# Turning the summed probabilities of two key blocks instead of each one

## The chip, the cores and the metric

The kernel runs on one core of a Trainium2 chip. The metric is the time of the device in microseconds (us), the median of several runs. A profiled execution gives the rows shown here; in them PE is TensorE (PEld its weight loads), DVE is VectorE, ACT is ScalarE, POOL is GpSimd and SP issues DMAs.

## The reference

Three parts follow each other. The first is attention with a sliding window of 128 keys and 4 sink keys, over 4 batches x 8 heads, 768 positions, 64 columns a head:

```python
rel = pos[:, None] - pos[None, :]
keep = (pos[None, :] < n_sink) | ((rel >= 0) & (rel < window))
a = softmax(where(keep, scale * q @ k.T, -1e9))
x = a @ v                                   # to 3072 tokens x 512
h = x @ w_in;  x = (h * cos(h)) @ w_out     # 512 -> 2048 -> 512
```

Then a top-1 mixture of 8 experts: each token is routed by `argmax(x @ w_gate + bias)`, goes through `relu(x @ w1[e]) @ w2[e]` (512 to 1024 to 512) of its expert, and is scaled by its gate.

## The kernel before, in words

**Attention.** It is cut into 8 half-sequences (`hb`; `half = hb % 2`, the batch is `hb // 2`) of 384 queries, and each of these into 4 pairs of heads (`pr`). A half-sequence has three tiles `t` of 128 queries. A query's window lies in two neighbouring blocks of 128 keys: of the earlier block the keys behind a diagonal count, of its own block those up to the diagonal, so that the two parts are opposite triangles. Sixteen columns for the sinks stand between them: a tile of probabilities `Pb[t][j]` (`j` is the head of the pair) is `[earlier block 128 | sinks 16 | own block 128]`, 272 wide (`SEG` = 144, `W3` = 272). The first tile of a first half has no earlier block, and in the second tile of a first half (and in the first one) the sinks are within the blocks, by the masks with index 0 and 1.

`attn_front` loads q, k and v and turns q and k (`pq`, `pk`). Its `mid` makes the scores on TensorE (`ps`), adds the mask and takes the maximum on VectorE (L512), and exponentiates on ScalarE (L528), which also gives the row sums `sm`. Its `rest` scales `Pb` by 1/sum from the third half-sequence on (`whole`; L140 on VectorE, and on GpSimd for `hb` = 2), turns each 128x128 block with TensorE against the identity into the PSUM tile `pt` (L551 the earlier block, L552 the own one), and ScalarE copies `pt` to `pT` in SBUF (L554). The sinks' columns are gathered (`pc`), turned (`pz`) and copied (`sp`). Then `po` gathers the product with v: block by block of keys, two tiles of queries at a time, `pT` as the moving operand. ScalarE and VectorE part `po` into a high and a low half, `xT_h` and `xT_l`.

**The feed-forward part.** It works on the half-sequences one step behind: for each of 16 column blocks `f` twelve matmuls make `hp` (L136), VectorE and ScalarE make `ch` = h cos h from it, ScalarE the high half `g_h`, GpSimd the low half `g_l`, and nine matmuls add to `y` (L622). `hp` has two PSUM banks.

**The order.** Attention and feed-forward are generators. Each `yield` of attention returns a weight, and `run_ffn` advances the other generator by it. A scheduler then sets the order on each engine from this order and its own picture of durations. PSUM tiles named by `ps_a` (`pq`, `pk`, `ps`, `pt`, `pz`, `po`, `yT` and others) share a few banks in turn, so that a new one waits until the reader of an old one is done. Each engine executes its queue in order. The mixture of experts follows from about 800 us on, after the routing; it is not touched.

Of the kernel before, what the change touches and what calls it, by code (L numbers as in the profile page):

```python
# [13 lines left out]
BF16 = DT.bfloat16  # L14
# [3 lines left out]
ALU = mybir.AluOpType  # L18
AX = mybir.AxisListType

P = 128
# [40 lines left out]
def kernel(  # L62
# [30 lines left out]
    SEG = P + NS  # L93
    W3 = 2 * P + NS
# [7 lines left out]
    PE, ACT, DVE, POOL, SP = nc.tensor, nc.scalar, nc.vector, nc.gpsimd, nc.sync  # L102
# [30 lines left out]
    const = ctx.enter_context(tc.tile_pool(name="const", bufs=1))  # L133

    def mm(o, l, r, start, stop):
        PE.matmul(o, l, r, start=start, stop=stop)  # L136

    def ts(e, o, i, s1, op0, s2=None, op1=None):
        if op1 is None:
            e.tensor_scalar(out=o, in0=i, scalar1=s1, scalar2=None, op0=op0)  # L140
        else:
            e.tensor_scalar(out=o, in0=i, scalar1=s1, scalar2=s2, op0=op0, op1=op1)  # L142
# [4 lines left out]
    def tt(e, o, a, b, op):  # L147
        e.tensor_tensor(out=o, in0=a, in1=b, op=op)  # L148


    ident = const.tile([P, P], F32, name="ident")
# [162 lines left out]
    def steps(hb):  # L314
        return STEPS_0 if hb <= 1 else STEPS_1
# [80 lines left out]
    def attn_front(hb, pr):  # L396
        b, half = divmod(hb, 2)
# [3 lines left out]
        extra = hb <= EX and pr % 2 == 1  # L401

        whole = hb > EX
        vs_n, sp = vs_n2[pr % 2], sp2[pr % 2]
        n_ps = [0]

        def psb(name):
            if hb > 0 or not extra:
                return ps_a(name)
            n_ps[0] += 1  # L410
            return ps_y(n_ps[0] % NQ, name)
# [119 lines left out]
        def rest():  # L531
            xh, xl = xT[hb]
            for t in range(NQ if whole else 0):
                ts(DVE, sm[:, 2 * t:2 * t + 2], sm[:, 2 * t:2 * t + 2], 1e-9, ALU.add)
                DVE.reciprocal(sm[:, 2 * t:2 * t + 2], sm[:, 2 * t:2 * t + 2])
                for j in range(2):
                    c0, c1, _ = cols(t)
                    i = 2 * t + j
                    if hb < NPOOL:
                        ts(POOL, Pb[t][j][:, c0:c1], Pb[t][j][:, c0:c1], sm[:, i:i + 1], ALU.mult, 0.0, ALU.add)  # L540
                    else:
                        ts(DVE, Pb[t][j][:, c0:c1], Pb[t][j][:, c0:c1], sm[:, i:i + 1], ALU.mult)
            yield steps(hb)[3]
            pT = apool.tile([P, 2, NQ * 256], F32, name="pT", bufs=2)
            for t in range(NQ):
                pt = psb("pt").rearrange("p (j x) -> p j x", j=2)
                first = half == 0 and t == 0
                s0 = P if first else 0
                for j in range(2):
                    if not first:  # L550
                        PE.transpose(pt[:, j, 0:P], Pb[t][j][:, 0:P], ident)  # L551
                    PE.transpose(pt[:, j, P:2 * P], Pb[t][j][:, SEG:W3], ident)  # L552
                o_ = slice(t * 256 + s0, (t + 1) * 256)
                ACT.activation(out=pT[:, :, o_], in_=pt[:, :, s0:256], func=AF.Copy)  # L554
                yield steps(hb)[4]
            if not whole:

                ts(DVE, sm, sm, 1e-9, ALU.add)
                DVE.reciprocal(sm, sm)
                rb = [pb_x[t + NQ * (pr % 2)][:, 3 * P:4 * P] for t in range(NQ)]  # L560
                for t in range(NQ):
                    POOL.tensor_copy(rb[t].rearrange("p (j d) -> p j d", d=D),
                                     sm[:, 2 * t:2 * t + 2].unsqueeze(2).to_broadcast([P, 2, D]))
            t0 = 2 if half == 0 else 0
            pc = apool.tile([P, NQ, 2, NS], F32, name="pc")
            if extra:
                for t in range(t0, NQ):
                    for j in range(2):
                        POOL.tensor_copy(pc[:, t, j], Pb[t][j][:, P:SEG])
            else:  # L570
                (POOL if hb < NPOOL else DVE).tensor_copy(pc[:, t0:], Pt[:, t0:, :, P:SEG])
            pz = psb("pz")
            for t in range(t0, NQ):
                PE.transpose(pz[0:2 * NS, t * P:(t + 1) * P], pc[:, t].rearrange("p j s -> p (j s)"), ident)
            ACT.activation(out=sp[0:2 * NS, t0 * P:], in_=pz[0:2 * NS, t0 * P:HALF], func=AF.Copy)
            yield steps(hb)[5]
            def band(blk):

                own = blk if half == 0 else blk - 1
                ta, tb = max(own, 0), min(own + 1, NQ - 1)  # L580
                c0 = ta * P
                c1 = (tb + 1) * P
                m0 = own * 256 + P if own >= 0 else 0
                return c0, c1, m0, m0 + (c1 - c0)

            po = psb("po")
            for j in range(2):
                mm(po[hr[j], t0 * P:HALF], vs_n[:, j * D:(j + 1) * D], sp[:, t0 * P:HALF], True, False)
            for blk in range(nblk):
                c0, c1, m0, m1 = band(blk)  # L590
                for j in range(2):
                    mm(po[hr[j], c0:c1], vn[:, blk, j, :], pT[:, j, m0:m1], False, blk == nblk - 1)
            yield 2 * nblk * steps(hb)[6]
            if whole:
                ACT.activation(out=xh[:, pr, :], in_=po[:, 0:HALF], func=AF.Copy)
                tt(DVE, xl[:, pr, :], po[:, 0:HALF], xh[:, pr, :].bitcast(F32), ALU.subtract)
            else:
                pf = psb("pf")
                for t in range(NQ):
                    mm(pf[:, t * P:(t + 1) * P], rb[t], ident, True, True)  # L600
                xs = apool.tile([P, HALF], F32, name="xs")
                ACT.activation(out=xs, in_=pf[:, 0:HALF], func=AF.Copy)
                tt(DVE, xs, po[:, 0:HALF], xs, ALU.mult)
                ACT.activation(out=xh[:, pr, :], in_=xs, func=AF.Copy)
                tt(POOL, xl[:, pr, :], xs, xh[:, pr, :].bitcast(F32), ALU.subtract)
            for dst, x_ in ((xg_h, xh), (xg_l, xl)):
                SP.dma_start(out=x_[:, pr, :].bitcast(F32), in_=dst[half, b * H + h0:b * H + h0 + 2].rearrange("j d q -> (j d) q"), cond=bad_r > 0, cond_hint=False)
            yield steps(hb)[7]
# [274 lines left out]
    rel = tmpc.tile([P, P], F32, name="rel")  # L883
# [15 lines left out]
    DVE.tensor_copy(masks[:, 2, P:SEG], sk[:, 0:NS])  # L899
    ts(DVE, masks, masks, -1.0, ALU.add, -NEG / SCALE, ALU.mult)  # L900

    tri = const.tile([P, P], BF16, name="tri")
    ones = const.tile([P, P], BF16, name="ones")
    ts(DVE, tri, rel, 0.0, ALU.is_lt)
# [80 lines left out]
    for hb in range(1, NTILE):  # L985
# [8 lines left out]
        whole = attn_weight(hb) * ATT_STEPS[hb % 2] * (S_FIRST if hb == 1 else 1.0)  # L994
# [31 lines left out]
    for nm in ("xT_h", "xT_l"):  # L1026
        t = xpool.tile([P, KD, 256], F32R, name="m_" + nm, tag=nm)
# [354 lines left out]
```

## Time and profile before

| | |
|---|---|
| median of 3 runs | 1171.07 us (1166.01 to 1171.22) |
| profiled execution | 1171.1 us, its span 1169.0 us |
| TensorE busy | 1114.0 us, 95% of the span |
| VectorE, ScalarE, GpSimd busy | 683.7, 654.2, 224.8 us |
| DMA | 118.56 MB, mean 101 GB/s |

Busy time is an average over the stages: conversion of weights and the first two half-sequences until about 120 us, attention with feed-forward until about 700 us, the rest of the feed-forward part until about 830 us, and the experts. The duration of a matmul in a row overlaps the next one, so the distance between starts tells its cost. A time given behind a row in brackets, or behind the second bar of a group, is idle time of its engine just before, with the instruction that ended it.

### The profile page before, as it was taken

The page shows a single profiled execution, that of the slowest core. Times are in us where ns is not written, and L with a number is a line of the kernel's source. Part 1 is how long each engine was busy: PE and PEld are TensorE (multiplying, and loading weights), DVE is VectorE, ACT ScalarE, POOL GpSimd, SP SyncE. Part 2 cuts the span into 40 slices and gives each one's busy share as a digit, 9 for nine tenths or more (in the row PEclk, how much of TensorE's full clock was granted, in tenths as well). Part 3 has the DMA queues.
Part 4 walks back from the last instruction along what each step waited for, and adds up shares of the span by engine and source line. Part 5 has one row for each costly group of instructions (what it writes and reads, how often), then busy time and mean ns, then how long its engine had stood idle before and what let it go on. Part 6 is the DMA issues. An engine that isn't in the chain of part 4 may idle for free. (4 is left out here: it accounts for less than half of the span.)

```text
span 1169.0 us, 20954 instructions
## 1 busy us (share of the span) xinstructions
PE 1114.0 (95%) x6600; PEld 952.8 (82%) x6600; DVE 683.7 (58%) x2108; ACT 654.2 (56%) x1333; POOL 224.8 (19%) x275
## 2 busy tenths in 40 slices
PE   5989899999999999999999999999999998999994
PEld 3667677888888888887888889899889996899983
DVE  6668699765777766777687664746741224522210
ACT  4798778776686767776677762444222224422221
POOL 1223133311111111111111112221112211121110
PEclk9999899999999999999999999999999998999998
DMA  7475575433423333352343323623151115121110
GB/s 162 116 213 166 160 217 171 114 83 86 100 67 95 108 90 80 84 107 73 85 107 84 86 65 112 238 75 109 40 195 57 56 38 181 29 62 42 40 48 16
DMA packets 139285, 118.56 MB, mean 101 GB/s; under 512 B 96367, under 2 KB 105583, under 8 KB 139120
## 3 DMA queue, kind: packets, MB, share of 16 engines
q1 hardware_dynamic: 134800, 103.02, 31.6%
q0 software_dynamic: 4320, 13.65, 3.6%
q8 instruction: 65, 1.06, 0.4%
q14 instruction: 100, 0.82, 0.2%
HBM read 151.06 MB, written 19.67 MB: 146 GB/s over the span
## 5 line engine op out<-in xcount | busy, mean ns | idle before, releaser
L148 POOL TENSOR_TENSOR g_l<-ch,g_h 128x384 fp32r<-128x384 f32 x128 | 131.9, 1031 | 564.4 <-ACT g_h L694 512.4
L136 PE MATMUL hp<-xT_h,wi_h 128*128 128x384 f32 x512 | 181.4, 355 | 1.8 <-DVE ch L148 1.8
L136 PE MATMUL hp<-xT_h,wi_l 128*128 128x384 f32 x512 | 175.4, 343 | 0.0
L136 PE MATMUL hp<-xT_l,wi_h 128*128 128x384 f32 x512 | 175.0, 342 | 0.0
L622 PE MATMUL y<-wo,g_h 128*128 128x512 f32 x384 | 157.7, 411 | 0.0
L622 PE MATMUL y<-wo_l,g_h 128*128 128x512 f32 x384 | 156.1, 406 | 0.0
L622 PE MATMUL y<-wo,g_l 128*128 128x512 f32 x384 | 155.0, 404 | 0.2 <-POOL g_l L148 0.2
L684 ACT ACTIVATE ch<-ch,cols 128x384 f32<-128x384 f32 x128 | 78.9, 616 | 106.5 <-DVE ch L145 105.8
L136 PE MATMUL m_y<-wi_h,hT 128*128 128x512 f32 x416 | 132.5, 393 | 0.7 <-ACT m_ot L1128 0.5
L145 DVE SCALAR_TENSOR_TENSOR hT<-m_h,hT 128x256 fp32r<-128x256 f32 x88 | 37.4, 425 | 152.7 <-ACTq L1280 102.6
L142 DVE TENSOR_SCALAR ch<-hp 128x384 int32<-128x384 f32 x128 | 71.2, 556 | 64.7 <-PE hp L136 50.5
L136 PEld LDWEIGHTS hp<-xT_h,wi_h 128*128 128x128 f32 x512 | 96.9, 190 | 10.3 <-issue 3.8
L136 PEld LDWEIGHTS hp<-xT_l,wi_h 128*128 128x128 f32 x512 | 97.3, 190 | 5.7 <-issue 2.5
L694 ACT ACTIVATE g_h<-ch 128x384 fp32r<-128x384 f32 x128 | 66.7, 521 | 56.9 <-DVE ch L148 39.1
L136 PEld LDWEIGHTS hp<-xT_h,wi_l 128*128 128x128 f32 x512 | 96.9, 189 | 2.0 <-issue 1.9
L148 DVE TENSOR_TENSOR ch<-ch,hp 128x384 f32<-128x384 f32 x128 | 70.5, 551 | 43.7 <-ACT ch L684 43.2
L136 PEld LDWEIGHTS m_y<-wi_h,hT 128*128 128x128 f32 x416 | 78.0, 188 | 16.9 <-issue 0.9
L528 ACT ACTIVATE Pb<-Pb,mx 128x272 f32<-128x272 f32 (+1 forms) x168 | 82.9, 495 | 7.7 <-DVE mx L512 7.2
L622 PEld LDWEIGHTS y<-wo,g_l 128*128 128x128 f32 x384 | 72.5, 189 | 14.8 <-POOL g_l L148 0.9
L1097 ACT ACTIVATE hT<-m_h 128x256 fp32r<-128x256 f32 x88 | 34.0, 387 | 89.4 <-PE m_h L136 80.5
L136 PE MATMUL ps<-kT,qT 64*128 64x272 f32 (+3 forms) x264 | 71.1, 379 | 10.5 <-ACT kT L475 10.3
L136 PE MATMUL m_y<-wi_l,hT 128*128 128x512 f32 x208 | 81.0, 390 | 0.0
(275 smaller groups left out, 2413.5 us busy)
## 6 DMA issues: line engine op xcount, KB each, us to landing
rw<-in_moe_w_dram SPq DMA_DIRECT2D x112, 512.0 KB
wo_l<-wl_scr SPq DMA_DIRECT2D x122, 256.0 KB
cv_in<-in_moe_w_in_dram SPq DMA_DIRECT2D x16, 512.0 KB
cv_out<-in_moe_w_out_dram SPq DMA_DIRECT2D x16, 512.0 KB
y_scr<-yt SPq DMA_DIRECT2D x24, 256.5 KB
xT_h<-xg_h SPq DMA_DIRECT2D x32, 192.0 KB
xT_l<-xg_l SPq DMA_DIRECT2D x32, 192.0 KB
qn<-in_q_dram SPq DMA_DIRECT2D x56, 96.0 KB
```

The source lines that it names most:

```text
L136: PE.matmul(o, l, r, start=start, stop=stop)
L142: e.tensor_scalar(out=o, in0=i, scalar1=s1, scalar2=s2, op0=op0, op1=op1)
L145: e.scalar_tensor_tensor(out=o, in0=i0, scalar=s, in1=i1, op0=op0, op1=op1)
L148: e.tensor_tensor(out=o, in0=a, in1=b, op=op)
L528: ACT.activation(out=Pb[t][j][:, c0:c1], in_=Pb[t][j][:, c0:c1], func=AF.Exp, scale=-1.0, bias=mx[:, i:i + 1], accum_out=sm[:, i:i + 1])
L622: i = PE.matmul(o, l, r, start=start, stop=stop)
L684: ACT.activation(out=ch, in_=ch, func=AF.Sin, scale=TWO_PI, bias=half_pi)
L694: ACT.activation(out=gh, in_=ch, func=AF.Copy)
L1097: ACT.activation(out=hT_h[f], in_=hp, func=AF.Relu)
```

## The change

A tile is *folded* if its window has two whole blocks and its sinks lie in the 16 columns alone: every tile of a second half, and the third one of a first half, from the third half-sequence on. For such a tile VectorE first adds the earlier block into the own block for both heads at once; the scaling then covers only the sinks and that sum, 144 columns instead of 272; TensorE turns one block a head instead of two; and VectorE, in ScalarE's place, writes both triangles to `pT` by multiplying the turned sum, read twice, with the 0/1 masks `sides`. These are made once at the start, by two instructions on VectorE. The layout of `pT` and what reads it stay as they were, and so do the weights that the yields return.

```diff
@@ -401,6 +401,10 @@
         extra = hb <= EX and pr % 2 == 1
 
         whole = hb > EX
+
+        def folded(t):
+            return whole and (half == 1 or t > 1)
+
         vs_n, sp = vs_n2[pr % 2], sp2[pr % 2]
         n_ps = [0]
 
@@ -533,8 +537,12 @@
             for t in range(NQ if whole else 0):
                 ts(DVE, sm[:, 2 * t:2 * t + 2], sm[:, 2 * t:2 * t + 2], 1e-9, ALU.add)
                 DVE.reciprocal(sm[:, 2 * t:2 * t + 2], sm[:, 2 * t:2 * t + 2])
+                if folded(t):
+                    tt(DVE, Pt[:, t, :, SEG:W3], Pt[:, t, :, SEG:W3], Pt[:, t, :, 0:P], ALU.add)
                 for j in range(2):
                     c0, c1, _ = cols(t)
+                    if folded(t):
+                        c0 = P
                     i = 2 * t + j
                     if hb < NPOOL:
                         ts(POOL, Pb[t][j][:, c0:c1], Pb[t][j][:, c0:c1], sm[:, i:i + 1], ALU.mult, 0.0, ALU.add)
@@ -546,6 +554,16 @@
                 pt = psb("pt").rearrange("p (j x) -> p j x", j=2)
                 first = half == 0 and t == 0
                 s0 = P if first else 0
+                if folded(t):
+                    pt2 = pt[:, 0]
+                    for j in range(2):
+                        PE.transpose(pt2[:, j * P:(j + 1) * P], Pb[t][j][:, SEG:W3], ident)
+                    s4 = [P, 2, 2, P]
+                    tt(DVE, pT[:, :, t * 256:(t + 1) * 256].rearrange("p j (x q) -> p j x q", x=2),
+                       pt2.rearrange("p (j q) -> p j q", j=2).unsqueeze(2).to_broadcast(s4),
+                       sides.unsqueeze(1).to_broadcast(s4), ALU.mult)
+                    yield steps(hb)[4]
+                    continue
                 for j in range(2):
                     if not first:
                         PE.transpose(pt[:, j, 0:P], Pb[t][j][:, 0:P], ident)
@@ -899,6 +917,9 @@
     DVE.tensor_copy(masks[:, 2, P:SEG], sk[:, 0:NS])
     ts(DVE, masks, masks, -1.0, ALU.add, -NEG / SCALE, ALU.mult)
 
+    sides = const.tile([P, 2, P], BF16, name="sides")
+    ts(DVE, sides[:, 0], rel, 0.0, ALU.is_gt)
+    ts(DVE, sides[:, 1], rel, 0.0, ALU.is_le)
     tri = const.tile([P, P], BF16, name="tri")
     ones = const.tile([P, P], BF16, name="ones")
     ts(DVE, tri, rel, 0.0, ALU.is_lt)
```

How this moves instructions is shown at three places. The first is TensorE in the second pair of the sixth half-sequence (a second half), from the last turn of the pair (`pt`) to its product with v (`po`). Before:

```order
L551 MATMUL pt<-ident,Pb_5459 128x128
L552 MATMUL pt<-ident,Pb_5459 128x128
L551 MATMUL pt<-ident,Pb_5459 128x128
L552 MATMUL pt<-ident,Pb_5459 128x128
L574 MATMUL pz<-ident,pc 32x128 x2
L622 MATMUL y_5388<-wo_114,g_h 128x512
...
L622 MATMUL y_5390<-wo_l,g_h 128x512
L622 MATMUL y_5390<-wo_114,g_l 128x512
L136 MATMUL po<-sp_139,vs_n_137 64x384 x2
L136 MATMUL po<-pT,vn 64x128 x2
L136 MATMUL po<-pT,vn 64x256 x4
```

And now (`y` and `hp` are matmuls of the feed-forward part):

```order
L560 MATMUL pt<-ident,Pb_5439 128x128 x2
L640 MATMUL y_5369<-wo_l,g_h 128x512
...
L640 MATMUL y_5370<-wo_114,g_l 128x512
L136 MATMUL hp<-xT_h,wi_h_85 128x384
...
L592 MATMUL pz<-ident,pc 32x128 x3
L136 MATMUL hp<-xT_h,wi_h_85 128x384
...
L136 MATMUL hp<-xT_h,wi_l_95 128x384
L136 MATMUL po<-sp_139,vs_n_137 64x384 x2
L136 MATMUL po<-pT,vn 64x128 x2
L136 MATMUL po<-pT,vn 64x256 x4
```

Two turns stand where there were four. Between the last turn and `po` stand five matmuls of `y`, nine of `hp` and the turns `pz` of the sinks' columns, where there were nine of `y` and two of the turns `pz`.

The second place is VectorE's queue in the same pair, up to `xT_l`, the low half of `po`. Before:

```order
L148 TENSOR_TENSOR kl_2752<-pk,kT 64x4x128
L140 TENSOR_SCALAR Pb_5459<-Pb_5459,sm 128x272 x2
L571 COPY pc<-Pb_5459 128x96
L148 TENSOR_TENSOR ch<-ch,hp 128x384
L148 TENSOR_TENSOR qT<-pq,qT 64x384
L148 TENSOR_TENSOR kl_2754<-pk,kT 64x4x128
L142 TENSOR_SCALAR ch<-hp 128x384
L145 SCALAR_TENSOR_TENSOR ch<-hp,ch 128x384
L148 TENSOR_TENSOR ch<-ch,hp 128x384
L148 TENSOR_TENSOR xT_l<-po,xT_h 128x384
```

And now (`pT<-pt,sides` is the product with the mask):

```order
L539 RECIPROCAL sm<-sm 128x2
L148 TENSOR_TENSOR pT<-pt,sides 128x2x256
L140 TENSOR_SCALAR Pb_5439<-Pb_5439,sm 128x144 x2
L148 TENSOR_TENSOR ch<-ch,hp 128x384
L148 TENSOR_TENSOR qT<-pq,qT 64x384
L148 TENSOR_TENSOR kl_2754<-pk,kT 64x4x128
L148 TENSOR_TENSOR pT<-pt,sides 128x2x256 x2
L142 TENSOR_SCALAR ch<-hp 128x384
L589 COPY pc<-Pb_5439 128x96
L145 SCALAR_TENSOR_TENSOR ch<-hp,ch 128x384
L148 TENSOR_TENSOR ch<-ch,hp 128x384
L148 TENSOR_TENSOR xT_l<-po,xT_h 128x384
```

The three products have come in between the scaling, `qT` and `kl`, and stand ahead of the last `ch` steps.

The third is VectorE at the start of the program, up to the first scores with their mask (`Pb,mx<-ps,masks`). Before:

```order
L148 TENSOR_TENSOR masks<-mw,sk 128x128
L148 TENSOR_TENSOR bias_all<-bias_all,btmp 128x192
L142 TENSOR_SCALAR mw<-rel,lim 128x128
L142 TENSOR_SCALAR tok_236<-iota_f 128x24
L142 TENSOR_SCALAR e_239<-iota_f 128x8
L897 CAST masks<-mw 128x128
L148 TENSOR_TENSOR masks<-mw,sk 128x128
L477 COPY kT<-pk 128x2x16
L142 TENSOR_SCALAR masks<-masks 128x816
L140 TENSOR_SCALAR tok_236<-tok_236,cols_198 128x24
L140 TENSOR_SCALAR cv_a<-cv_h 128x512
L512 ISA Pb,mx<-ps,masks 128x128
```

And now:

```order
L140 TENSOR_SCALAR sides<-rel 128x128
L142 TENSOR_SCALAR mw<-rel,lim 128x128
L140 TENSOR_SCALAR tri<-rel 128x128
L915 CAST masks<-mw 128x128
L148 TENSOR_TENSOR masks<-mw,sk 128x128
L481 COPY kT<-pk 128x2x16
L142 TENSOR_SCALAR masks<-masks 128x816
L148 TENSOR_TENSOR bias_all<-bias_all,btmp 128x192
L140 TENSOR_SCALAR cv_a<-cv_h 128x512
L140 TENSOR_SCALAR tok_239<-tok_239,cols_198 128x24
L145 SCALAR_TENSOR_TENSOR cv_a<-cv_h,cv_a 128x512
L516 ISA Pb,mx<-ps,masks 128x128
```

One of the two instructions for `sides` is seen here (the other stands six rows earlier), and a second step of the weights' conversion, `cv_a`, has come ahead of the first scores. Behind this place the order differs on all engines in small steps, up to about 216 us, although the work there is the same.

## Rows read from the trace of the kernel before

**Rows 1.** The page: busy us and instructions by engine; granted TensorE clock by slice.
```profile
PE 1114.0 (95%) x6600; PEld 952.8 (82%) x6600; DVE 683.7 (58%) x2108; ACT 654.2 (56%) x1333; POOL 224.8 (19%) x275
...
PEclk9999899999999999999999999999999998999998
```

**Rows 2.** Windows table by stage: busy us (instructions) by engine, granted clock, DMA.
```profile
core 0: us, PE busy (x) PEld busy (x) DVE busy (x) ACT busy (x) POOL busy (x), PEclk, DMA share, GB/s
0.00:120.00 120.00, 100.44 (x583) 70.98 (x583) 85.00 (x264) 89.75 (x217) 28.93 (x69) 1.00 0.60 164
120.00:216.00 96.00, 92.85 (x471) 71.13 (x471) 78.78 (x198) 74.98 (x153) 29.93 (x44) 0.95 0.63 180
216.00:316.00 100.00, 98.29 (x595) 84.84 (x595) 68.13 (x224) 71.28 (x137) 17.00 (x17) 1.00 0.35 89
452.00:484.00 32.00, 31.99 (x201) 26.78 (x201) 19.38 (x55) 21.55 (x41) 6.04 (x6) 1.00 0.32 86
120.00:700.00 580.00, 569.18 (x3355) 481.97 (x3355) 416.16 (x1322) 420.98 (x830) 111.20 (x124) 0.99 0.39 103
```

**Rows 3.** Order of time on TensorE around four turns: start us, us, instruction.
```profile
450.09 0.39 PE L622 MATMUL y<-wo,g_l 128*128 128x512 f32 x1
450.32 0.27 PE L551 MATMUL pt<-ident,Pb 128*128 128x128 f32 x1
...
450.65 0.27 PE L552 MATMUL pt<-ident,Pb 128*128 128x128 f32 x1
...
450.94 0.34 PE L136 MATMUL hp<-xT_l,wi_h 128*128 128x384 f32 x1
451.11 0.34 PE L136 MATMUL hp<-xT_h,wi_l 128*128 128x384 f32 x1
```

**Rows 4.** Waits of TensorE's weight loads, 210 to 700 us: total us, times, longest.
```profile
PEld pt L551 <- DVE kl L148: 6.2, 7, 1.0
...
PEld pt L551 <- ACT pT L554: 3.7, 9, 0.8
...
PEld po L136 <- ACT sp L575: 1.9, 6, 0.4
...
PEld pt L551 <- DVE qT L148: 1.2, 1, 1.2
```

**Rows 5.** Two windows, and two rows of TensorE in order of time, 118 to 140 us.
```profile
120.00:125.00 5.00, 5.00 (x17) 3.46 (x17) 4.84 (x19) 4.92 (x7) 0.00 (x0) 0.64 0.94 265
125.00:130.00 5.00, 5.00 (x20) 4.33 (x20) 1.73 (x5) 4.96 (x15) 1.73 (x3) 0.68 0.17 40
...
119.51 0.49 PE L136 MATMUL ps<-kT,qT 64*128 64x128 f32 x4 [1.72 <-ACT kT L475]
...
134.41 0.45 PE L136 MATMUL hp<-xT_h,wi_h 128*128 128x384 f32 x1 [1.77 <-DVE ch L148]
```

**Rows 6.** Groups by form: shapes and count, busy us, mean ns, idle before.
```profile
L554 ACT ACTIVATE pT<-pt 128x512 f32<-128x512 f32 x80 | 47.1, 594 | 9.3 <-PE pt L552 7.5
...
L148 DVE TENSOR_TENSOR kl<-pk,kT 64x512 fp32r<-64x512 f32 x24 | 16.5, 689 | 0.8
...
L148 DVE TENSOR_TENSOR ch<-ch,hp 128x384 f32<-128x384 f32 x128 | 70.5, 551 | 43.7 <-ACT ch L684 43.2
...
L140 DVE TENSOR_SCALAR Pb<-Pb,sm 128x272 f32<-128x272 f32 x104 | 34.4, 361 | 0.9
...
L140 DVE TENSOR_SCALAR Pb<-Pb,sm 128x128 f32<-128x128 f32 x16 | 4.2, 282 | 0.1
```

**Rows 7.** The page's group of GpSimd; tile Pb on VectorE, ns min/median/max.
```profile
L148 POOL TENSOR_TENSOR g_l<-ch,g_h 128x384 fp32r<-128x384 f32 x128 | 131.9, 1031 | 564.4 <-ACT g_h L694 512.4
...
L140 DVE TENSOR_SCALAR Pb<-Pb,sm x120: 277/356/878, 226.7 to 692.8; 128x272 f32<-128x272 f32 x104, 128x128 f32<-128x128 f32 x16
```

**Rows 8.** Order of time on VectorE at the start.
```profile
11.20 0.22 DVE L140 TENSOR_SCALAR tri<-rel 128x128 bf16<-128x128 f32 x1
...
13.98 0.28 DVE L512 CUSTOM_DVE_ANT_0 Pb<-ps,masks 128x128 f32<-128x128 f32 x1
```

## The prediction

> **What bounds the kernel now.** I began with the page's busy shares and slices [rows 1]. TensorE is busy 1114.0 of 1169.0 us and VectorE 683.7; the reader should see that the slices of PE stand at 8 and 9 nearly throughout, so that the question is stage by stage whether anything but TensorE is late. The table of windows [rows 2] cuts the span at the half-sequences of attention. The change works in the six of them that run from about 120 to 700 us. In that stretch TensorE is busy 569.18 of 580.00 us. The window from 452 to 484 us, in the middle of a second half, has 31.99 of 32.00: there a TensorE instruction taken away is time taken away. VectorE has 68.13 of 100.00 us in the second half at 216 to 316 us, ScalarE 71.28. The stage before, 120 to 216 us, is the tight one for VectorE, with 78.78 of 96.00 us. Before 120 us nothing is folded, but TensorE idles about 20 us there.
>
> Next I read the order of time on TensorE around four turns [rows 3]: what one costs is the distance from start to start, not its duration of 0.27 us. From the first to the fourth turn it is 450.65 - 450.32 = 0.33 us in three steps, 0.11 us each. From the matmul ahead to the second one behind it is 450.94 - 450.09 = 0.85 us, which is 0.23 for y, 0.44 for four turns and 0.18 for hp: no price for going in and out of the group is left over.
>
> Then the waits of the weight loads, which is where TensorE's queue stops first [rows 4]. From 210 to 700 us it waited 6.2 + 1.2 = 7.4 us for VectorE and 3.7 + 1.9 = 5.6 us for ScalarE. Last, the one place where the granted clock falls in the stages that matter [rows 5]: after a wait of 1.72 us that ends at 119.51, the next 10 us have a clock of 0.64 and 0.68 instead of 1.00, which loses 5 x 0.36 + 5 x 0.32 = 3.4 us; with its wait this event costs 5.1 us. A second wait, 1.77 us for VectorE's ch at 134.41, stands a little behind. Both are in the stage where VectorE is fullest.
>
> **The change part by part.** Folded are t = 2 of the first halves and all three t of the second ones, from the third half-sequence on: 4 pairs x (3 x 1 + 3 x 3) = 48 tiles of queries.
>
> *TensorE.* Each folded tile has two turns where there were four. 48 x 2 x 0.11 = 10.6 us less. The windows say that nearly all of it is on the path: the idle share of TensorE from 120 to 700 us is 10.8 of 580 us. The Trainium skill ("TensorE: Matmul & The Clock Gate", Part 4: PE-mode transpose) gives some 275 ns for a turn in a kernel's context; the trace has that as the duration and 110 ns as the spacing. By the page's figure the turns would be worth 96 x 0.275 = 26.4 us and the whole sum would come to 1148 us, an estimate that I don't follow, since the starts in the trace show that turns overlap.
>
> *ScalarE* loses 48 copies of pt at 0.594 us, 28.5 us [rows 6]. None is on the path by itself; it shortens the ScalarE part of the waits.
>
> *VectorE* takes them over. The product with the mask, 512 wide out of PSUM, is not in the trace with a bf16 operand; its nearest row is kl, 512 wide from PSUM with another operand in SBUF, at 689 ns. The sum is 256 wide: by 384 wide at 551 and 512 at 689 a further 128 columns cost 138 ns, so some 413 ns. The scaling shrinks from 272 to 144 columns: 361 - 282 = 79 ns for 144, so 70 ns for 128, 88 times on VectorE (8 more are on GpSimd). Together 48 x 0.69 + 48 x 0.41 - 88 x 0.07 = 33.1 + 19.7 - 6.2 = 46.6 us. From 216 to 700 us VectorE has 416.16 - 78.78 = 337.4 of 484 us, 70%; with 44 of the 48 tiles it goes to 379 of about 474, 80%. ScalarE goes from 71% to 67%. In 120 to 216 us VectorE goes from 82% to 87%. So it stays under TensorE in each stage, and what the 46.6 us cost is only the waits that they add.
>
> How much? In the pair that the order shows, po stands behind the last turn by 5 matmuls of y and 9 of hp, 5 x 0.23 + 9 x 0.17 = 2.7 us, while VectorE has two products left, 1.4 us: 1.3 us to spare. Behind these products in VectorE's queue stand pc, ch and then xT_l, so a late product also holds back the chain of the feed-forward part, which has two hp banks of cover. The lower end is that the ScalarE waits go and none comes, -5.6 us; the upper is that each of the 24 pairs takes a wait like those for kl now, 6.2 / 7 = 0.9 us, so +21 us. I take +3: the VectorE waits of 7.4 us grow with its load (80 / 20 against 70 / 30 is 1.7 times, +5) and the ScalarE ones shrink (67 / 33 against 71 / 29, -1), and the 32 us that have no wait for VectorE at all pull it down.
>
> A sum in SBUF may also be held by GpSimd. The trace has this: scaling on VectorE has a median of 356 ns and a longest of 878, and GpSimd's g_l takes 1031 ns each [rows 7]. With GpSimd busy 17% of the time it is a part of the spread above and not a term. The Trainium skill says why ("SBUF — State Buffer", Who interferes with whom): an operation of VectorE with two inputs in SBUF and one of GpSimd that reads SBUF exclude each other for a whole instruction. The row agrees that something of half a microsecond exists; by the page's rule the worst case would be 48 x 1.03 = 49 us more on VectorE, an estimate that would need every sum to begin just behind a g_l.
>
> *The start.* Two mask instructions stand on VectorE before the scores' masks are done; tri, of the same shape, takes 0.22 us [rows 8]. A step of the weight conversion now also stands ahead of the first Pb at 13.98 us, where TensorE waits for it. Two masks are 0.44 us; I take +0.5, between 0 and 1.2 (the conversion is only moved). From there on the order on all engines is another one up to 216 us, with the same work in it; I take 0 for that, and -8.6 to +8.6 as its bounds: the two events of rows 5 (5.1 us, and 1.77 us of wait with, by half the first one's loss, 1.7 us of slow clock) go, or two such are added.
>
> The sum, on the profiled execution's own 1171.1 us (span 1169.0 and 2.1 around it; the median of the runs is 1171.07, the same): 1171.1 - 10.6 + 3 + 0.5 = 1164.0 us.
>
> **The rivals.** *A, slower: po waits for VectorE.* The product of the last tile is late in most pairs, because the sum and three products now stand in one queue with ch, qT, kl and yT. For it: kl on VectorE is already what the turns wait for most. Against: the 1.3 us to spare in the order, and ScalarE freed of 2 us just before sp. At 0.9 us in each of 24 pairs it is 1171.1 - 10.6 + 0.5 + 21.3 = 1182 us. It begins to decide at 10.6 / 24 = 0.44 us a pair, that is when the product starts 1.7 us late.
>
> *B, no change: the new order of the first 216 us costs what the turns give.* Two more events like those of rows 5 are 8.6 us: 1172.6. For it: VectorE at 87% there, with a wait for it already. Against: the work is the same but for 4 us on VectorE.
>
> *C, more: the new order loses these two events*, 1164 - 8.6 = 1155 us. ScalarE, the releaser of the first wait, has no less to do there, so this is the less likely direction.
>
> That the change does nothing because the removed turns lay in idle time can be ruled out by 31.99 of 32.00.
>
> **How the numbers follow.** Forecast 0.53, with its own range of 1158 to 1170; A 0.15; B 0.20; C 0.12. About 0.5%, 5.9 us, is what a measurement of this kernel can tell from no change, so faster means below 1165.2 and slower above 1176.9. Of the forecast's 0.53 some 0.39 lie below 1165.2 and 0.14 within; with C faster is 0.51, with B no change is 0.34, and A is slower, 0.15. For 8 in 10 the range takes in C's end and B and leaves most of A out: 1155 to 1176.
>
> **What would show it.** The TensorE matmuls fall by 96, with 0.11 us from start to start of the turns that are left; the stages 216 to 316 and 410 to 510 us, with 12 folded tiles, become 2 to 2.6 us shorter each, the first halves 0.4 to 0.9. The product with sides shows 0.69 us and the sum 0.41. VectorE's share from 216 to 700 us shows 80%. Wrong it is if po or pz waits for pT by more than 0.44 us a pair (A), or if the time until 216 us is more than 4 us off in either direction (B, C). If the product takes over 0.8 us or the sum over 0.6, the load of VectorE was mis-sized.

## The result, and the profile after

The changed kernel takes 1150.1 us (median of 4 runs, 1148.45 to 1153.6), the kernel before beside it 1168.54 (4 runs, 1165.32 to 1171.22): ratio 0.9842, 95% interval 0.9818 to 0.9866. The forecast was 1164, its range 1155 to 1176. The direction was right; the time came out 14 us under the forecast and 5 us under the range. The profiled execution is 1149.4 us, its span 1147.6.

The page of the changed kernel, busy time by engine and granted clock by slice:

```profile
PE 1093.7 (95%) x6504; PEld 936.0 (82%) x6504; DVE 716.4 (62%) x2206; ACT 629.4 (55%) x1283; POOL 224.8 (20%) x275
...
PEclk9999999999999999999999999999999999999998
```

The 96 matmuls are gone, and VectorE has 716.4 us instead of 683.7 [rows 1]. New is the clock. It has two levels, 1.00 (2.4 GHz) and 0.50 (1.2 GHz); a number between them is a stretch with some of both. Both dents of the kernel before [rows 1] are gone, the one in the fifth slice and the one in the 34th (964 to 994 us, in the experts).

Windows table of the changed kernel, columns as in [rows 2]:

```profile
0.00:120.00 120.00, 101.69 (x589) 72.25 (x591) 87.33 (x277) 90.69 (x222) 29.16 (x69) 0.99 0.63 172
120.00:216.00 96.00, 92.99 (x509) 73.02 (x507) 80.74 (x211) 75.79 (x155) 31.50 (x46) 1.00 0.61 177
216.00:316.00 100.00, 97.32 (x585) 83.45 (x584) 79.08 (x260) 66.97 (x129) 16.42 (x16) 1.00 0.35 90
...
120.00:125.00 5.00, 5.00 (x30) 4.24 (x28) 4.78 (x14) 4.94 (x11) 0.00 (x0) 1.00 0.66 193
125.00:130.00 5.00, 4.23 (x26) 3.60 (x25) 4.34 (x14) 4.97 (x11) 4.50 (x8) 1.00 0.89 259
...
216.00:700.00 484.00, 472.04 (x2826) 406.25 (x2825) 373.44 (x1208) 325.01 (x631) 83.05 (x82) 1.00 0.36 92
```

Between 120 and 216 us TensorE now gets 509 matmuls into the window in which it had 471 [rows 2], and the two stretches from 120 to 130 us, which had a clock of 0.64 and 0.68 [rows 5], have 1.00. VectorE is at 373.44 of 484 us, 77%.

The new operations on VectorE, groups by tile with ns min/median/max:

```profile
L148 DVE TENSOR_TENSOR pT<-pt,sides x48: 665/684/694, 130.6 to 682.2; 128x512 f32<-128x512 f32 x48
...
L140 DVE TENSOR_SCALAR Pb<-Pb,sm x120: 277/290/852, 217.8 to 678.4; 128x144 f32<-128x144 f32 x88, 128x128 f32<-128x128 f32 x16, 128x272 f32<-128x272 f32 x16
L148 DVE TENSOR_TENSOR Pb<-Pb x48: 398/417/433, 126.7 to 676.9; 128x256 f32<-128x256 f32 x48
```

The product takes 684 ns, where kl's 689 [rows 6] had stood in for it; the sum 417, for which 413 was worked out.

TensorE in order of time around the two turns of one tile:

```profile
442.03 0.39 PE L640 MATMUL y<-wo,g_h 128*128 128x512 f32 x1
442.26 0.38 PE L560 MATMUL pt<-ident,Pb 128*128 128x128 f32 x2
442.39 0.48 PE L640 MATMUL y<-wo_l,g_h 128*128 128x512 f32 x1
442.71 0.39 PE L640 MATMUL y<-wo,g_l 128*128 128x512 f32 x1
```

From y to the second y behind it are 0.68 us, of which 2 x 0.23 belong to y: 0.22 for two turns, 0.11 each, as in [rows 3].

Waits of the weight loads in the changed kernel, 200 to 690 us:

```profile
PEld pt L560 <- ACT kT L472: 5.1, 6, 0.9
PEld po L136 <- ACT sp L593: 4.6, 15, 0.6
...
PEld pt L560 <- ACT qT L453: 2.5, 3, 0.9
PEld pt L560 <- DVE kl L148: 2.2, 2, 1.1
PEld pt L569 <- DVE kl L148: 2.0, 2, 1.0
PEld pt L560 <- ACT pT L572: 1.8, 2, 0.9
```

kl is waited for less than before [rows 4], sp more. No row of this view has po or pz waiting for pT.

Where the 21.4 us between the two spans are is read from ScalarE's copies, which end each part of the work; the starts of the copies are the marks. In the changed kernel (order of time, ScalarE; the last copy of the first, second and seventh feed-forward tile, then copies of expert results):

```profile
137.69 0.60 ACT L730 ACTIVATE y_part<-y 128x512 f32<-128x512 f32 x1 [0.70 <-DMA yp_scr<-y_part]
...
226.65 0.60 ACT L742 ACTIVATE yt<-y 128x512 f32<-128x512 f32 x1
...
698.46 0.59 ACT L742 ACTIVATE yt<-y 128x512 f32<-128x512 f32 x1
...
959.95 0.69 ACT L1149 ACTIVATE m_ot<-m_y,m_yg 128x512 f32<-128x512 f32 x1 [4.70 <-PE m_y L136]
...
980.33 0.68 ACT L1149 ACTIVATE m_ot<-m_y,m_yg 128x512 f32<-128x512 f32 x1
...
1005.00 0.69 ACT L1149 ACTIVATE m_ot<-m_y,m_yg 128x512 f32<-128x512 f32 x1 [4.70 <-PE m_y L136]
...
1121.64 0.69 ACT L1149 ACTIVATE m_ot<-m_y,m_yg 128x512 f32<-128x512 f32 x1 [4.70 <-PE m_y L136]
...
1135.30 0.69 ACT L1149 ACTIVATE m_ot<-m_y,m_yg 128x512 f32<-128x512 f32 x1 [2.49 <-PE m_y L136]
```

The same in the kernel before, its first four:

```profile
143.97 0.58 ACT L712 ACTIVATE y_part<-y 128x512 f32<-128x512 f32 x1
...
236.25 0.59 ACT L724 ACTIVATE yt<-y 128x512 f32<-128x512 f32 x1
...
713.68 0.59 ACT L724 ACTIVATE yt<-y 128x512 f32<-128x512 f32 x1
...
975.64 0.69 ACT L1128 ACTIVATE m_ot<-m_y,m_yg 128x512 f32<-128x512 f32 x1 [4.70 <-PE m_y L136]
```

These cut the span into: **S**, up to the first row (the start, up to 144 us before); **F1**, to the second row; **F2**, to the third (477 us before); **R**, to the fourth; **X**, three places of the experts: from the fourth row to the sixth (tile 6, which is not full, and the tile behind it) and from the seventh to the eighth (tile 13, not full). The changed kernel has S 137.69, F1 226.65 - 137.69 = 88.96, F2 698.46 - 226.65 = 471.81, R 959.95 - 698.46 = 261.49, X 45.05 + 13.66 = 58.71. For every kernel of this study, worked out from its profile in the same way (us; the rest of the experts is 128.4 to 129.5 in all). A profiled execution lies at most 2.1 us from the median of its kernel's runs, but that of e2 is its fastest, 4.5 us under the median:

| kernel | S | F1 | F2 | R | X | span |
|---|---|---|---|---|---|---|
| before | 143.97 | 92.28 | 477.43 | 261.96 | 63.90 | 1169.0 |
| e4, before again | 141.44 | 92.02 | 477.15 | 261.57 | 64.47 | 1165.9 |
| e13, before, 32 skipped turns | 141.70 | 92.38 | 477.19 | 261.66 | 59.06 | 1160.6 |
| e14, before, 64 skipped turns | 144.90 | 92.84 | 477.21 | 261.67 | 59.49 | 1165.0 |
| e1, before with the masks | 139.22 | 92.68 | 476.61 | 262.19 | 62.08 | 1161.9 |
| e8, four turns, product | 137.17 | 89.31 | 479.41 | 261.99 | 63.60 | 1160.5 |
| e2, folded, old start | 142.67 | 88.86 | 471.70 | 261.30 | 57.63 | 1151.6 |
| e7, folded, ScalarE copies | 137.23 | 91.18 | 471.36 | 261.51 | 61.36 | 1151.0 |
| after | 137.69 | 88.96 | 471.81 | 261.49 | 58.71 | 1147.6 |
| e3, after again | 135.92 | 88.83 | 471.69 | 261.36 | 60.17 | 1147.3 |
| e12, after again | 135.74 | 88.72 | 471.71 | 261.36 | 60.36 | 1146.4 |
| e9, after, 32 skipped turns | 139.63 | 88.56 | 471.62 | 261.29 | 60.15 | 1150.7 |
| e10, after, 64 | 137.79 | 88.77 | 471.67 | 261.39 | 63.64 | 1152.5 |
| e5, after, 96 | 140.08 | 88.71 | 471.66 | 261.59 | 64.40 | 1155.0 |
| e6, after, 96 at tile 6 | 137.53 | 88.88 | 471.68 | 261.62 | 65.29 | 1154.2 |
| e11, after, 128 | 137.73 | 88.84 | 471.69 | 261.26 | 62.31 | 1150.9 |

Of the 21.4 us, S gave 6.3, F1 3.3, F2 5.6 and X 5.2. All folded tiles but one of the 48 lie in F1 and F2. More than half of the gain lies in S, where the work is the same but for two mask instructions and that one tile, and in X, which the change does not touch.

### The profile page after: what moved, and what is told of

It is laid out like the page before. It is cut to its first block, busy times and chain, and to the rows that moved or that the text cites. A ratio compares the mean times of both kernels' runs of the same rounds, so it can differ in the third digit from the quotient of the medians.

```text
span 1147.6 us, 20806 instructions
## 1 busy us (share of the span) xinstructions
PE 1093.7 (95%) x6504; PEld 936.0 (82%) x6504; DVE 716.4 (62%) x2206; ACT 629.4 (55%) x1283; POOL 224.8 (20%) x275
## 4 chain that ended last, share of the span: by engine, by line
PE 76%; DVE 12%; ACT 4%; DMA 4%; issue 2%; POOL 1%; SPq 0%; DVEq 0%; POOLq 0%; ACTq 0%
PE hp L136 19%; PE y L640 18%; PE m_y L136 10%; PE m_h L136 10%; PE po L136 5%; PE ps L136 4%; DMA out_dram<-m_ot,m_ids 3%; PE pl L768 1%; DVE pT L148 1%; DVE qT L148 1%; DVE ch L142 1%; DVE kl L148 1%; PE m_a L1107 1%; PE pq L445 1%; PE pt L570 1%
## 5 line engine op out<-in xcount | busy, mean ns | idle before, releaser
L640 PEld LDWEIGHTS y<-wo,g_h 128*128 128x128 f32 x384 | 72.4, 189 | 10.5 <-issue 2.7
```

Source lines behind the costliest of these rows:

```text
L640: i = PE.matmul(o, l, r, start=start, stop=stop)
```

## The experiments

**Two by two: the start's order and the folding.** e1 is the kernel before with the two mask instructions, which nothing reads; this gives the start the changed kernel's order, on TensorE for the first 643 matmuls, up to 132 us. e2 is the changed kernel with the masks made on GpSimd, which leaves TensorE's start as it was before for 640 matmuls, up to 135 us. e3 and e4 are the two kernels again.

```diff
e1, against before
+    sides = const.tile([P, 2, P], BF16, name="sides")
+    ts(DVE, sides[:, 0], rel, 0.0, ALU.is_gt)
+    ts(DVE, sides[:, 1], rel, 0.0, ALU.is_le)
e2, against after
-    ts(DVE, sides[:, 0], rel, 0.0, ALU.is_gt)
-    ts(DVE, sides[:, 1], rel, 0.0, ALU.is_le)
+    ts(POOL, sides[:, 0], rel, 0.0, ALU.is_gt, 0.0, ALU.add)
+    ts(POOL, sides[:, 1], rel, 0.0, ALU.is_le, 0.0, ALU.add)
```

> The kernel before with the two mask instructions on VectorE at the start and nothing folded: 96 turns more than the changed kernel, but its order of instructions on all engines for the first two half-sequences. Theory 1, that a part of the gain is the new order which these two instructions bring about: between 1168.5 - 9 and 1168.5 - 5, so 1160 to 1164 us, with the first feed-forward tile's partial results copied out near 137.7 us (144.0 before) and a granted clock of 1.00 from 120 to 216 us (0.95 before). Theory 2, that the whole gain comes from the folded tiles: 1168 to 1170 us, since two masks cost about 0.4 us.

> The changed kernel with its two masks made by GpSimd, so that VectorE's queue and the order of the first two half-sequences are those of the kernel before; the folding is all there. Theory 1: the folding alone is worth 10.6 us of turns less 3 to 5 us of added waits, so 1160 to 1163 us, with 144 us for the first partial results. Theory 2: 1150 us, as the changed kernel. If both E1 and this one stay near 1168, the gain would be an interaction of the two.

> The changed kernel as it is, for a second profile. Its last 380 us, the experts, took 5.5 us less in the profiled execution than in that of the kernel before, with the same code. If that is a matter of the single execution (theory 1), its time from the last feed-forward copy (768 us) to the end will differ by 1 to 4 us from the first profile's 377.5 us; if it belongs to the change, it stays at 377 to 378 us. Time 1149 to 1152 us by either.

> The kernel before as it is, for a second profile: ratio 1.00. By theory 1 the time from the last feed-forward copy (784 us) to the end differs from the first profile's 383.4 us, and lies between 378 and 384 us; if the longer experts' part belongs to this kernel, it stays at 383 to 384 us. The slow clock between 119 and 140 us should show again by either theory, since it follows waits that the order sets.

Measured, beside 1169.96 us for before: e1 1162.02, ratio 0.9934 (0.9917 to 0.9951); e2 1157.85, 0.9891 (0.9871 to 0.9911); e3 1149.47, 0.9829 (0.981 to 0.9848); e4 1170.07, 0.9997 (0.9983 to 1.0011). The two parts add up: -8.0 and -12.1 against -20.5 for both. e1 came out as its first theory had it. e2 lies 2 us under the 1160 to 1163 us of that theory: turns less waits are not all of its gain, and its X, 57.63 us, is the shortest of all. The repeats say that the shorter time of the experts is not the chance of one execution: from the last copy of y to the end the changed kernel takes 377.6 us and in e3 379.1, the kernel before 383.4 both times.

What the new order does in the start is seen in TensorE's waits from 12 to 145 us (total us, times, longest). Before:

```profile
PE ps L136 <- ACT kT L475: 10.3, 4, 7.0
PE pf L136 <- ACT kT L475: 2.3, 1, 2.3
PE hp L136 <- DVE ch L148: 1.8, 1, 1.8
```

And e1:

```profile
PE ps L136 <- ACT kT L475: 7.2, 1, 7.2
PE hp L136 <- DVE ch L148: 2.4, 1, 2.4
PE ps L136 <- DVE mx L512: 1.4, 2, 1.1
PE pt L551 <- DVE mx L512: 1.0, 2, 0.6
```

Three of the four waits of the scores ps for ScalarE's kT are gone, and that of pf. Not all of this is gained, as the order of time tells. TensorE at the wait of pf before, and at the wait for ch in e1:

```profile
71.64 0.68 PE L136 MATMUL pf<-ident,pb_x 128*128 128x128 f32 x4 [2.30 <-ACT kT L475]
...
69.80 0.44 PE L136 MATMUL hp<-xT_h,wi_h 128*128 128x384 f32 x1 [2.36 <-DVE ch L148]
```

Here one wait has taken the place of another. What is gone are the two waits of rows 5, 1.72 us for kT at 119.51 and 1.77 us for ch at 134.41. All five profiles with the old order have both, 1.72 to 1.98 us each; in the eleven with the new order no wait between 75 and 145 us is longer than 0.95 us. With the two waits went the slow clock behind them. A third window of the kernel before shows it behind the second wait, as rows 5 do behind the first:

```profile
135.00:140.00 5.00, 5.00 (x23) 4.45 (x22) 2.33 (x5) 5.00 (x11) 1.01 (x1) 0.66 0.30 85
```

And windows of e1, where before had 0.64 and 0.68 [rows 5]:

```profile
120.00:125.00 5.00, 5.00 (x26) 4.02 (x26) 4.51 (x14) 4.94 (x12) 0.00 (x0) 1.00 0.90 251
125.00:130.00 5.00, 4.48 (x26) 3.51 (x25) 4.38 (x14) 4.96 (x10) 2.47 (x4) 1.00 0.79 220
```

S bears it out over all the profiles: 141.4 to 144.9 us in the five with the old order, 135.7 to 140.1 in the eleven with the new one, means 142.9 and 137.8, 5 us apart. The clock from 120 to 145 us is 1.00 in each of the eleven, and in each of the five it falls somewhere between 120 and 140 us. How much it falls differs from one execution to the next with the same two waits: e4 has 0.73 and 0.93 in the windows of rows 5 and 1.00 behind the second wait. The rest of e1's 8.0 us is not of the start: its X is 2 us shorter too, with a tile behind the first single one that took 24.7 us where before took 26.0 (both occur in executions of one kernel).

**What the folding gains: the turns or ScalarE's time.** e8 takes the sum out: four turns, 272 columns scaled, VectorE's product in ScalarE's place. e7 takes the product off VectorE: ScalarE copies the turned sum twice, without the masks.

```diff
e8, against after
-                if folded(t):
-                    tt(DVE, Pt[:, t, :, SEG:W3], Pt[:, t, :, SEG:W3], Pt[:, t, :, 0:P], ALU.add)
...
-                    if folded(t):
-                        c0 = P
...
-                    pt2 = pt[:, 0]
...
-                        PE.transpose(pt2[:, j * P:(j + 1) * P], Pb[t][j][:, SEG:W3], ident)
+                        PE.transpose(pt[:, j, 0:P], Pb[t][j][:, 0:P], ident)
+                        PE.transpose(pt[:, j, P:2 * P], Pb[t][j][:, SEG:W3], ident)
...
-                       pt2.rearrange("p (j q) -> p j q", j=2).unsqueeze(2).to_broadcast(s4),
+                       pt.rearrange("p j (x q) -> p j x q", x=2),
e7, against after
-                    tt(DVE, pT[:, :, t * 256:(t + 1) * 256].rearrange("p j (x q) -> p j x q", x=2),
-                       pt2.rearrange("p (j q) -> p j q", j=2).unsqueeze(2).to_broadcast(s4),
-                       sides.unsqueeze(1).to_broadcast(s4), ALU.mult)
+                    ACT.activation(out=pT[:, :, t * 256:(t + 1) * 256].rearrange("p j (x q) -> p j x q", x=2),
+                                   in_=pt2.rearrange("p (j q) -> p j q", j=2).unsqueeze(2).to_broadcast(s4), func=AF.Copy)
```

> The changed kernel without the sum: four turns a tile as before, 272 columns scaled, and VectorE multiplies both blocks by the masks, so ScalarE is relieved as in the changed kernel and TensorE is not. Theory (the gain of folding is the turns): what the two mask instructions gave stays, the 10.6 us of turns are not saved, and VectorE's product adds 0 to 3 us: 1161 to 1165 us, a ratio of 0.993 to 0.996. Rival (the gain of folding came from ScalarE's 28.5 us less): 1151 to 1156 us, 0.984 to 0.988.

> The changed kernel with the product taken off VectorE: ScalarE copies the turned sum twice instead. The masks are not applied, so the two triangles are not parted. Theory (VectorE's 48 products of 0.68 us lie beside TensorE's work and cost at most 2 us of waits): the same time as the changed kernel or up to 2 us less, 1147.5 to 1149.5 us, a ratio of 0.981 to 0.983. Rival (the +3 us that the forecast set for VectorE's waits are there, and more of the 10.6 us of the turns was lost to them): 1144 to 1146 us, 0.978 to 0.980.

e8: 1162.88 us beside 1170.24, ratio 0.9939 (0.9919 to 0.9958), the same as e1. Its copies of y (order of time, ScalarE):

```profile
226.48 0.60 ACT L738 ACTIVATE yt<-y 128x512 f32<-128x512 f32 x1
...
705.89 0.59 ACT L738 ACTIVATE yt<-y 128x512 f32<-128x512 f32 x1
```

So F2 is 479.41 us with four turns and 471.81 with two: 7.6 us. Against e1, the product alone costs 2.8 us in F2 and gives 3.4 in F1, where ScalarE was fuller, so it is about nothing; the turns with the sum then give 7.6 + 0.35 = 8.0 of their 10.6 us. e7: 1153.08 us, 0.985 (0.9816 to 0.9884), no faster than the changed kernel; its F2 is 471.36 and its F1 2.2 us longer. That is above the time of either of its theories, which both had it as fast or faster. VectorE's product therefore costs no more than ScalarE's copy would, and the rival of both runs is out.

**The experts.** X was the surprise. TensorE stands idle ahead of the two tiles that are not full, where it passes over the branch for a full tile; the profile calls this wait "issue". Before, e4 and e1 have 5.39, 5.19 and 4.95 us there, after, e3 and e2 3.34, 3.24 and 2.75. The kernel before (order of time, TensorE):

```profile
980.99 0.77 PE L136 MATMUL m_h<-wi_h,m_xT_h 128*128 128x512 f32 x1 [5.39 <-issue]
...
1143.12 0.47 PE L136 MATMUL m_h<-wi_h,m_x 128*128 128x512 f32 x1 [2.02 <-issue]
```

The changed kernel:

```profile
963.26 0.76 PE L136 MATMUL m_h<-wi_h,m_xT_h 128*128 128x512 f32 x1 [3.34 <-issue]
...
1122.21 0.47 PE L136 MATMUL m_h<-wi_h,m_x 128*128 128x512 f32 x1 [0.61 <-issue]
```

The instructions are the same; what differs is that TensorE's program is 96 turns shorter ahead of them (e2, e3 and the changed kernel have 6504 matmuls, the others 6600). So turns were put back where nothing executes them: in the branch for a not-full tile of expert tile 1 (e5; 32, 64 and 128 of them in e9, e10 and e11), or in the branch for a full tile of tile 6 (e6). The order of all engines is otherwise the same, row by row.

```diff
e5, against after, in the branch that tile 1 passes over
-            ahead(rows_and_gather if after is not None else None)
+            ahead(rows_and_gather if after is not None else None); _ = [PE.transpose(m_h[0][:, 0:P], ident, ident) for _ in range(96 if T == 1 else 0)]
e6, against after, in the branch that tile 6 passes over
-            second_product(T, 1, m_y[1], None, after)
+            second_product(T, 1, m_y[1], None, after); _ = [PE.transpose(m_h[0][:, 0:P], ident, ident) for _ in range(96 if T == 6 else 0)]
```

> The changed kernel with 96 turns added to the branch for a not-full tile of expert tile 1, a branch that is passed over. Nothing more is executed, and the order on all engines is the same, but TensorE's code behind that place lies as far along as in the kernel before. Theory (the place of the code decides how soon TensorE gets its next instructions when it passes over a branch): the wait <-issue ahead of the first not-full tile grows from about 3.3 us to the 5 us of the kernel before, and the one ahead of the last tile from 0.6 to 2 us; with the slow clock behind them the time is 3 to 5 us longer than the changed kernel's, 1153 to 1155 us, a ratio of 0.985 to 0.988. Rival (something else in the folded kernels makes these waits shorter, or chance does): 3.3 and 0.6 us again, 1149.5 us, 0.983.

> The changed kernel with the 96 turns in the branch of expert tile 6 for a full tile, which is passed over just there: the jump ahead of the first not-full tile is 96 turns longer, and the code behind it lies as far along as in the kernel before. By the place theory as in the run beside it, 5 us and 2 us of wait and 1153 to 1155 us; if the length of the jump decides and not the place, 5 us or more at this tile here and not in the run beside it; if neither does, 3.3 and 0.6 us and 1149.5 us, 0.983.

e5 takes 1157.04 us, ratio 0.9888 (0.9859 to 0.9916), e6 1155.98, 0.9879 (0.9848 to 0.9911), 1 to 2 us above the 1153 to 1155 expected; X is 64.40 and 65.29, as in the kernel before. The first wait of e6 is 5.84 us; e5 has such a wait too, with the turns elsewhere, so it does not take a longer jump. TensorE in e5:

```profile
966.75 0.77 PE L136 MATMUL m_h<-wi_h,m_xT_h 128*128 128x512 f32 x1 [4.75 <-issue]
...
1130.09 0.47 PE L136 MATMUL m_h<-wi_h,m_x 128*128 128x512 f32 x1 [1.94 <-issue]
```

The seven us behind the end of the first wait, in e5 and then in the changed kernel:

```profile
966.75:973.75 7.00, 7.00 (x19) 5.54 (x20) 2.80 (x5) 3.50 (x7) 0.45 (x1) 0.59 0.54 179
...
963.26:970.26 7.00, 7.00 (x25) 5.61 (x26) 3.85 (x7) 4.71 (x9) 1.02 (x1) 0.78 0.53 181
```

The wait comes back, and with it a longer stretch at the slow clock.

> The changed kernel with 32 turns instead of 96 in the skipped branch of tile 1. If the wait ahead of a not-full tile grows evenly with the place of the code, 3.3 + 1.5 / 3 = 3.8 us ahead of the first and 1.0 ahead of the last, and 1151 us. If the program is fetched in blocks, so that the place within a block decides, the wait need not lie between those of 0 and 96 turns; anything from 0 to 6 us.

> As the run beside it, with 64 turns. Evenly: 3.3 + 2 x 1.5 / 3 = 4.3 us and 1.5 us, 1153 us. By blocks: anything from 0 to 6 us.

> With 128 turns, 256 instructions. Evenly: 5.3 us and 2.4 us, and 1156 us or more. By blocks of 256 instructions, which is the size of the transfers in the page's instruction queue q8 (1.06 MB in 65 packets, 16 KB, if an instruction takes 64 bytes): the same place in a block as the changed kernel, 3.3 and 0.6 us, 1149.5 us.

> The changed kernel once more, to have it on the same chip as the three others: 3.2 to 3.4 us and 0.6 us of wait, 1149 to 1151 us, a ratio of 0.981 to 0.985.

On one chip, beside 1170.9 us for before: e12 1148.3 (0.9811, 0.9783 to 0.9838), e9 1152.67 (0.9837, 0.981 to 0.9864), e10 1154.11 (0.985, 0.9821 to 0.988), e11 1151.78 (0.9831, 0.9804 to 0.9858). The first waits are 3.14, 2.77, 3.83 and 3.70 us, X is 60.4, 60.2, 63.6 and 62.3. That is not even growth, since 128 turns cost less than 96. With 128 turns, 256 instructions, the two waits are 3.70 and 0.79 us, near the 3.14 to 3.34 and 0.61 to 0.99 of the place of none, as blocks of 256 instructions would have it, though not quite the same. Last, the kernel before was moved in the same way, by the same line with 32 and 64 turns:

> The kernel before with 32 turns added to the skipped branch of expert tile 1: nothing more is executed. TensorE's code behind it then lies where it does in the changed kernel with 128 turns added. If the place decides, this kernel has the waits of that one, 3.7 and 0.8 us instead of 5.2 to 5.4 and 2.0 to 2.3, and its two single tiles and the tile behind the first of them take 62 us together instead of 64; 1167 to 1169 us, a ratio of 0.997 to 0.999. Rival (the short waits come with the folding): 5.2 and 2 us, 64 us, a ratio of 1.000.

> The same with 64 turns, a place that none of the kernels had. If the place decides, the waits ahead of the single tiles differ from those of the kernel before by more than the 0.2 us by which its two executions differ, in either direction; the time then goes with them, 1165 to 1173 us. Rival: 5.2 and 2 us, 64 us, a ratio of 1.000.

e13 takes 1163.51 us, ratio 0.9958 (0.994 to 0.9975), e14 1166.21, 0.9978 (0.996 to 0.9996). TensorE in e13:

```profile
976.62 0.77 PE L136 MATMUL m_h<-wi_h,m_xT_h 128*128 128x512 f32 x1 [3.73 <-ACT wi_h L1040]
...
1135.71 0.47 PE L136 MATMUL m_h<-wi_h,m_x 128*128 128x512 f32 x1 [0.64 <-issue]
```

Both waits are those of e11, 3.7 and 0.8 us, as the place theory had it, and X falls to 59.06, below the 62 us that it gave; the time is 3.5 us under the 1167 to 1169 expected. In e14 the waits are 2.43 and 1.08 us, and X is 59.49. So the kernel before becomes faster by instructions that never run.

Sorted by the place of the code behind the skipped branch, counted in turns from that of the changed kernel and begun again at 128 (so that e11 and e13 stand at 0, e14 at 32, the kernel before at 96), the waits of all sixteen profiles fall in line (us):

| place | profiles | first wait | last wait | X |
|---|---|---|---|---|
| 0 | after, e2, e3, e7, e11, e12, e13 | 2.75 to 3.73 | 0.38 to 0.99 | 57.6 to 62.3 |
| 32 | e9, e14 | 2.77, 2.43 | 0.73, 1.08 | 60.2, 59.5 |
| 64 | e10 | 3.83 | 2.40 | 63.6 |
| 96 | before, e1, e4, e5, e6, e8 | 4.75 to 5.84 | 1.94 to 2.52 | 62.1 to 65.3 |

X is 59.9 us in the mean at place 0 and 64.0 at 96. Some 4 us of X thus belong to the place of TensorE's code and not to the folding: folded and unfolded kernels stand in both rows. That the places repeat after 128 turns was set out as one of two possibilities ahead of e11; for the other profiles it is read afterwards, and it was not tested further. At places 0 and 32 the code may not be what comes last: the profile ends the first wait by ScalarE's wi_h in e7, e13 and e14, and the last one by its m_ot in e3, e9, e11, e12 and e14.

No version here beats the changed kernel: of the five places tried for it, its own has the lowest time, though the interval of e9 (0.981 to 0.9864) overlaps that of e12.

## Why the prediction was wrong

**Where the step failed.** "From there on the order on all engines is another one up to 216 us, with the same work in it; I take 0 for that". Measured: e1 puts that order alone at -8.0 us, about 5 of it in S by the profiles. The bounds of 8.6 to either side held it, and rival C had the mechanism: both of its events went, each with its wait and the slow clock behind it. The windows of the kernel before lose 3.4 us behind the first wait, as the prediction had it, and 5 x 0.34 = 1.7 behind the second, which it had set by half the first one's loss. S fell by less than the 8.6 us of the two. Smaller waits came (0.45 and 0.75 us in the changed kernel between 75 and 145 us), its clock from 60 to 80 us is 0.91 where the kernel before had 1.00, and other executions lose less behind the same two waits: in e4 it is 5 x 0.27 + 5 x 0.07 = 1.7 us instead of 5.1. C was given 0.12, as "the less likely direction", on the ground that ScalarE, the first releaser, had no less to do. It had no less to do; the order of the same work sufficed. C's 1155 us was nearest, and the prediction's own sign for it came: the last copy of the second feed-forward tile starts at 226.65 instead of 236.25 us, more than 4 us off.

**What was not in the sum.** The experts, "not touched", gave 4 to 5 us by the place of the code. Nothing in the profile of before says that these waits can change; only moving the code showed it. Between the two profiles the sum lacked 21.4 - 7.1 = 14.3 us: 6.3 + 0.5 = 6.8 in S, 5.2 in X, 8.9 - 7.6 = 1.3 in F1 and F2, and 1.0 elsewhere.

**The turns, right.** 96 fewer, 0.11 us apart, 10.6 us. In the trace 8.0 of it is left between e8 and the changed kernel.

**The added waits, +3: right in size, only partly in kind.** Between e1 and the changed kernel F1 and F2 lose 3.7 + 4.8 = 8.5 us, so 2.1 of the 10.6 went to waits, and the sum for the folding alone was off by 1 us. But the 3 came from VectorE's waits growing by 5 and ScalarE's shrinking by 1. In the weight loads, where the prediction looked, it went the other way: the rows for VectorE add up to 7.4 us before [rows 4] and 6.7 now, those for ScalarE to 8.0 with the smaller rows and 14.6 now, for kT, sp and qT. What did grow for VectorE stands in TensorE's own waits, 130 to 690 us: 10.3 us, where it was 6.9 without the ch of rows 5. The new ones are turns that wait for the product of an earlier tile:

```profile
PE pt L560 <- DVE pT L148: 3.3, 6, 0.6
```

That the size came out is therefore partly luck.

**VectorE's load: the durations right, the sum too large.** The product takes 684 ns, the sum 417, and the scaling fell from 356 to 290 (medians). VectorE's busy time grew by 716.4 - 683.7 = 32.7 us and not by 46.6, because durations on VectorE overlap in part, as those of the turns do; rows 6 had it, with 104 scalings of 361 ns that are 34.4 us busy and not 37.5. So its share is 77% where 80 was forecast. GpSimd, rightly no term, did not lengthen the sum: its longest is 433 ns, with a median of 417.

**The stages, less than expected.** Between the last copies of y, the stages that end at 335, 529 and 714 us before, second halves, fell by 1.5, 2.3 and 1.1 us, where 2 to 2.6 were expected; the two first halves between them by 0.2 and 0.5, where it was 0.4 to 0.9.

**Rival A, out:** po never waited for pT (only the turns did), and 2.1 us in 24 pairs are 0.09 us each, where it decided from 0.44. **Rival B, out** in sign: the new order took events away.

**The Trainium skill's 275 ns a turn** ("TensorE: Matmul & The Clock Gate", Part 4: PE-mode transpose) had given 1148 us, close to the result, but not by its reason: e8 against the changed kernel puts the 96 turns with the sum at 8.0 us, 83 ns each, not 26 us.

## What to carry to other kernels

Split a gain by place before believing its cause: here only some 9 of 20 us came from the work that was removed. An instruction added at the start can reorder a hundred microseconds behind it, so do that edit alone, and the rest without it. And where the program branches late, move its code by skipped instructions before crediting a change with a few tenths of a per cent.

## What was not expected of the hardware

- Code that is never executed moved the time: 96 skipped turns cost the changed kernel about 0.6% (0.9888 and 0.9879 against 0.9829 and 0.9811), 32 made the kernel before 0.42% faster. X moved by 4 to 7 us. S of e5 and e9 is 2 to 4 us longer as well, but not by the moved code: e10 and e11, moved in the same way, have 137.8 and 137.7. In e5 and e9 the granted clock from 60 to 80 us is 0.83, where the changed kernel has 0.91, which is 1.6 us of it; what brought that about is not shown.
- How the place sets the wait is open. A wait that grows evenly with the place does not fit 2.77, 3.83, 4.75 and 3.70 us at 32, 64, 96 and 128 turns; places that repeat every 256 instructions sort all sixteen profiles, but no run shows why.
- A wait of 3 to 5 us at a branch costs more than itself: the granted clock over the 7 us behind it was 0.59 in e5 and 0.78 in the changed kernel. In e2, with 2.75 us, it was 1.00.
